# Two transposes moved from TensorE to DMA, statistics moved to ScalarE and a first chunk in halves, in a fused long-convolution and mixer kernel

## The chip, the core and the metric

The kernel runs on one core of a Trainium2 chip. The metric is the device time of one execution in microseconds (us). Several executions are timed on one chip, beside executions of the kernel before on the same chip. Each execution carries a state, fast or slow: slow, here, means that it was over 1.5% above the fastest of its own kernel. Ratios use fast executions alone and come with a 95% interval. A change counts as faster or slower when it is beyond 2%.

Names of engines: PE is TensorE (matmul), PEld its weight load, DVE VectorE, ACT ScalarE, POOL GpSimd, SP SyncE. In this kernel SP issues every DMA, so its program order is the order of all transfers.

## The reference

Two branches read the same `q`. Branch A is a long convolution of `k`, shifted and multiplied by `v`, with one filter of 2048 taps per channel (`ssm_k`, called h below). Branch B is a token mixer followed by a feed-forward network. S is 2048, D is 640, F is 1536; all is bf16.

```python
def _A_ref(q, k, v, shift_k, ssm_k, ssm_D):         # ssm_k: [D, S]
    ...                                              # k_shift: 4-tap shift of k
    kv = k_shift * v
    kv_f = rfft(pad(kv, 2*S));  kf_f = rfft(pad(ssm_k, 2*S))     # along S
    y = irfft(kv_f * kf_f)[:S] + kv * ssm_D
    return q * y
def _B_ref(x, w1, w2, w3, w4):
    h = gelu(layernorm(x) @ w1)
    ...                                              # 4 channel groups shifted by +1, -1, +2, -2 tokens
    x1 = x + hs @ w2
    return x1 + gelu(layernorm(x1) @ w3) @ w4
g = sigmoid((q * gate_w).sum(-1, keepdims=True))
out = g * _A_ref(...) + (1 - g) * _B_ref(q, ...)
```

## The kernel before

The kernel is written as a graph. Each node has a cost on the engines that can do it, its dependencies, and the buffers that it takes and gives back. A planner runs when the kernel is built: it simulates the graph with those costs, takes the ready node with the lowest key, and writes out one fixed order of instructions for each engine. On the chip every engine then works through its order; an instruction that is not ready holds all those behind it. The key is the longest path to the end plus a table of tuned shifts (`BIAS`).

```python
    def prepare(self):
        ...
            n.key = longest - n.rank + a + (b - a) * (k / (total[n.tag] - 1) if ... else 0.0)  # a, b from BIAS
    def forward(self):
        ...
                if n.bytes is not None:                      # a DMA: one line that all transfers share
                    line = max(now + 0.9, line) + n.bytes
                    fin = line + n.lat
                    ...
    def run(self):
        self.prepare()
        assert self.forward() is not None, "the plan is stuck"
        for n in sorted(self.nodes, key=lambda n: n.start):
            n.fn(n.engine)                                   # emitted once, in the planned order
SPILL = 3          # how many waiting copies let VectorE take one that ScalarE could do
BIAS = { ... }
```

The filter h arrives as [channel, time]; the transform wants time on the partitions. PE transposes it in five groups of 16, and ScalarE or VectorE copies each group out of PSUM:

```python
    for a in range(DT):                                       # DT = 5
        l_h.append(dma(lambda a=a: HNl[:, a, :], lambda a=a: hn_v[:, a, :], P * 4096, 4096, []))
    ...
        def f_ht(a=a, b=b):
            for t1 in range(T1):                              # T1 = 16
                nc.tensor.transpose(out=pt[:, t1 // 8, (t1 % 8) * P:(t1 % 8 + 1) * P], in_=HN[:, a, t1, :], identity=IDN[:])
        t = ten(pe(P, T1), [l_h[a], k_idn], f_ht, take=[b])
        ...                                                   # evac(...) copies to HT: the node k_ht
```

The table of the inverse transform (I1) is the transposed table of the forward one (F1), in 32 PE transposes:

```python
        def f_i1(h=h, b=b):
            for t1 in range(T1):
                nc.tensor.transpose(out=P16(b)[:, t1 // 8, (t1 % 8) * P:(t1 % 8 + 1) * P], in_=F1[:, t1, h, :], identity=IDN[:])
```

The statistics of the first normalization, one slab of 128 tokens at a time, are on VectorE. The first mixer product is 4 chunks of 512 tokens, five matmuls for each of five output tiles:

```python
            def f_st(s=s):
                for j in range(2):
                    nc.vector.bn_stats(out=BST[:, s % 4, j, :], in_=QX[:, s, j * DH:(j + 1) * DH])
                nc.vector.bn_aggr(out=MV[:, s, :], in_=BST[:, s % 4, :, :])
            ns.append(dvec(0.88, [l_q[s]], f_st))
    ...
                def f_w1(b=b, j=j, nt=n0 + j, xb=xb):
                    for k in range(DT):
                        nc.tensor.matmul(P32(b)[:, j, :], lhsT=lhsT, rhs=XNT[:, xb.slot, :, k, :], start=(k == 0), stop=(k == DT - 1))
```

The token shift of the mixer moves part of the activations between partitions' token slots by small DMAs (`mixsh`), and the last two of the ten matmuls of each slab of the second product (`W2`) read them.

Of the kernel before, what the change touches and what calls it, by code (L numbers as in the profile page):

```python
# [30 lines left out]
class Graph:  # L31
# [62 lines left out]
    def forward(self):  # L94
# [19 lines left out]
        while placed < len(nodes):  # L114
            while True:
                best = None
                for opts, q in queues.items():
# [5 lines left out]
                    if opts == "AV" and "A" not in es and len(q) + len(queues.get("A", ())) < self.spill:  # L123
                        continue
                    for item in sorted(q)[:24] if len(q) > 1 else q:
                        if all(len(free[p]) >= k for p, k in item[2].need):
                            if best is None or item[:2] < best[0][:2]:
                                best = (item, q, "A" if "A" in es else es[0])
                            break
# [51 lines left out]
SPILL = 3  # L181
BIAS = {
    "tA": (-1371, 329), "tF": (-1895.5, -724), "tM": (-895, -1806.5), "lq0": (-1748, -1584.5), "lq1": (-538.5, 1678),
    "lq2": (276.5, -148.5), "lq3": (-722.5, -2406.5), "lh0": (-599, -1171.5), "lh1": (-1262.5, 108), "lh2": (200, 76),
    "lh3": (-1543.5, -388), "lh4": (1371.5, 41), "lw1": (-813, 438.5), "lg5": (-966, -1374), "lsm": (933, 723.5),
    "halo": (630, 470), "lk0": (952.5, 1516.5), "lk1": (1326, -431.5), "lk2": (1247, 87.5), "lk3": (-844.5, -207.5),
    "lw2": (1010.5, 453), "pads": (-1392.5, -1903.5), "w1m": (-1378, -1422), "cj": (-2077.5, -1986.5),
    "hT0": (462, 872), "hT1": (-436.5, -54), "hT2": (-1567.5, -1321), "hT3": (-2415, -2453), "hT4": (-805, -1041),
    "LN1.4": (-1068.5, -2567), "LN1.5": (-1377.5, -101), "LN1.6": (1543, -177), "LN1.7": (694, 2098.5),
    "W1": (1173, 382), "W1.0": (-311.5, -391.5), "lv0": (930, 1060.5), "W1.1": (-908, -1017), "lv1": (2546.5, 2151),  # L190
    "W1.2": (-394.5, 484.5), "lv2": (-1163.5, -1804.5), "W1.3": (-365.5, 34.5), "lv3": (97.5, -194.5),
    "gate": (24.5, -1048.5), "mixsh": (-194.5, -1191.5), "W2": (-1393, -295.5), "ks": (-55, 124.5),
    "I1": (207.5, 486.5), "p0.1": (-514.5, -1036.5), "p0.gr": (-1858.5, -1351), "p0.2": (277.5, -1013),
    "p1.1": (85, -22.5), "p1.gr": (-1363.5, -97.5), "p1.2": (158, 494.5), "p2.1": (-1736.5, 232),
    "p2.hh": (-1426.5, -282), "p2.gr": (-1196.5, -1528), "p2.2": (43, -707), "p3.1": (242.5, 347),
    "p3.hh": (1072.5, 1036), "p3.gr": (-428.5, 985), "p3.2": (-2299.5, -1998), "qr": (-1357, -82),
    "inv0": (-194, 57.5), "inv1": (-1037.5, -824.5), "lw4": (-3682, -2611), "LN2": (-227, 584.5),
    "LN2.0": (-2078, -1915), "W3.0": (-910, -1875), "W4.0": (1205, 3183.5), "LN2.1": (-540.5, -382.5),
    "W3.1": (-347, 804.5), "W4.1": (545.5, 2369.5), "LN2.2": (-1716, -1532), "W3.2": (283, 624.5),
    "W4.2": (-1365, -2083.5), "LN2.3": (-1717.5, 551), "W3.3": (-793, 635.5), "W4.3": (1688.5, 488),  # L200
    "final": (-1560.5, -213.5),
# [11 lines left out]
def kernel(  # L213
# [47 lines left out]
    I1 = big.tile([P, 2, T1, P], BF16, name="I1")  # L261
# [9 lines left out]
    XD = dram.tile([4, T1, P, D], BF16, name="XD")  # L271
    HD = dram.tile([P + 64, T1, D], BF16, name="HD")
# [3 lines left out]
    HT = R3[:, 0].rearrange("p (e t d) -> p e t d", e=2, t=T1)  # L276
    KN = R3[:, 1].rearrange("p (t d) -> p t d", t=T1)
    HH = R3.rearrange("p a (t h d) -> p a t h d", t=T1, h=2)
    HN = R5.rearrange("p (a t2 t1) -> p a t1 t2", a=DT, t1=T1)
# [268 lines left out]


    k_ht = [[], []]  # L550
    for a in range(DT):
        G.tag = 'hT%d' % a
        b = G.buf("ps")

# [578 lines left out]
```

## Time and profile before

| before | us |
|---|---|
| median of 3 executions (lowest, highest) | 267.28 (266.84, 269.61) |
| the profiled execution, and its span | 265.0, 263.2 |
| PE busy, idle up to its last matmul at 259.24 | 237.3, 21.9 |
| first mixer matmul | 21.1 |
| first transform matmul that reads h | 29.8 |

The page of the profile first gives the busy time of each engine with its share of the span and its instructions, then strips of 40 slices (each 6.6 us) in which a digit is the busy share in tenths; `DMA` is the mean busy share of the 16 DMA engines. The line with percentages near the end is the chain of waits, followed back from the last instruction.

Windows of the kernel before. Columns: window, its length, then busy time and count of PE, PEld, DVE, ACT, POOL, then granted PE clock, DMA share, GB/s:

```profile
0.00:22.00 22.00, 9.13 (x73) 7.50 (x74) 19.77 (x66) 12.19 (x11) 15.49 (x35) 1.00 0.85 306
50.00:75.00 25.00, 24.05 (x183) 15.50 (x181) 23.25 (x40) 22.78 (x41) 7.83 (x18) 1.00 0.51 180
175.00:200.00 25.00, 23.57 (x149) 14.34 (x147) 10.25 (x13) 18.03 (x28) 0.00 (x0) 1.00 0.96 340
```

These three windows are the start, in which PE has 9.1 us of work; the middle of the mixer; and the third pass of the convolution.

The timeline of PE before. Columns: start, duration, engine, line, operation, output<-inputs, shapes, count; in brackets the idle time before it and what ended it:

```profile
7.09 1.93 PE L558 MATMUL ps_87<-IDN,R_71 128*128 128x128 bf16 x16 [7.09 <-DMA R_71<-in_A_ssm_k_dram]
...
21.10 2.84 PE L684 MATMUL ps_89<-XNT,R_75 128*128 128x512 bf16 x10
```

The first line is one of the five h groups of 16 transposes. It stands, with the next, in time in which PE has nothing else: of the 80 h transposes, part costs nothing. The last line is the start of the mixer.

### The profile page before, as it was taken

The numbers are of one execution on the slowest core, as the hardware profiler recorded it, in microseconds if no ns is written. First come the engines' busy times: TensorE is split into PE (matmuls) and PEld (weight loads), VectorE is DVE, ScalarE is ACT, GpSimd is POOL, SyncE is SP. The second block draws the span as 40 slices with busy tenths as digits, with TensorE's granted clock in tenths as the row PEclk, the third lists the DMA queues.
The fourth block names the chain that finished last, engine by engine and source line by source line (L and its number), as shares of the span: only waits on it lengthen the run. The fifth ranks groups of instructions, "written<-read, shape, count | busy, mean of one in ns | idle before, by whom it ended". The sixth has DMA issues, their size and how long they took to land.

```text
span 263.2 us, 4720 instructions
## 1 busy us (share of the span) xinstructions
PE 237.3 (90%) x1690; PEld 151.1 (57%) x1690; DVE 171.6 (65%) x340; ACT 184.3 (70%) x259; POOL 51.9 (20%) x115
## 2 busy tenths in 40 slices
PE   0549889999998899999999999997999999999993
PEld 0536446665665574555676555765556756756772
DVE  8999999889997799982111210364525444576995
ACT  2669969999889789989456789585877558753000
POOL 5894570061073585000000000000000000000000
PEclk9999999999999999999999999999999999999999
DMA  6994789944435996549899997999998572368874
GB/s 219 400 374 129 294 278 275 304 169 174 144 122 164 337 397 251 162 139 330 272 301 333 319 306 235 261 244 411 362 321 297 184 239 110 149 169 252 262 262 157
DMA packets 33601, 66.53 MB, mean 253 GB/s; under 512 B 5546, under 2 KB 22699, under 8 KB 33578
## 3 DMA queue, kind: packets, MB, share of 16 engines
q1 hardware_dynamic: 33578, 66.24, 76.3%
q8 instruction: 13, 0.21, 0.3%
q14 instruction: 10, 0.08, 0.1%
HBM read 40.79 MB, written 22.28 MB: 240 GB/s over the span
## 4 chain that ended last, share of the span: by engine, by line
PE 57%; DVE 16%; DMA 12%; ACT 7%; POOL 3%; issue 2%; SPq 1%; DVEq 0%; ACTq 0%
DMA VD<-HST 7%; PE ps_89 L1061 5%; PE ps_89 L1080 5%; DVE BST L590 4%; PE ps_88 L1061 4%; PE ps_90 L1080 4%; PE ps_90 L1061 4%; DMA XD<-SG 3%; DVE KV L990 3%; PE ps_90 L684 3%; PE ps_87 L1061 3%; ACT SG L351 2%; DVE QX L1097 2%; PE ps_87 L934 2%; PE ps_90 L780 2%
## 5 line engine op out<-in xcount | busy, mean ns | idle before, releaser
L1080 PEld LDWEIGHTS <-R_77 128*128 128x128 bf16 x384 | 37.6, 98 | 14.8
L923 DVE TENSOR_TENSOR PV<-XS,R_70 128x1280 bf16<-128x1280 bf16 x32 | 26.4, 824 | 28.4 <-PE ps_88 L934 12.0
L1061 PEld LDWEIGHTS <-R_75 128*128 128x128 bf16 x240 | 23.2, 98 | 21.0 <-issue 0.7
L809 DVE TENSOR_TENSOR R_72<-R_70,R_72 128x1280 bf16<-128x1280 bf16 (+3 forms) x32 | 23.9, 756 | 0.1
L1080 PE MATMUL ps_89<-R_72,R_77 128*128 128x320 bf16 x144 | 22.5, 299 | 0.0
L1080 PE MATMUL ps_90<-R_72,R_77 128*128 128x320 bf16 x144 | 21.8, 299 | 0.0
L812 DVE TENSOR_TENSOR R_72<-R_72 128x1280 bf16<-128x1280 bf16 x24 | 19.7, 823 | 0.5
L780 PEld LDWEIGHTS <-R_77 128*128 128x128 bf16 x160 | 15.6, 98 | 7.3 <-DMA R_77<-I_74 0.8
L1061 PE MATMUL ps_89<-XNT,R_75 128*128 128x512 bf16 x80 | 19.7, 379 | 0.0
L891 PEld LDWEIGHTS <-M_96 128*128 128x128 bf16 x128 | 12.3, 98 | 12.3 <-issue 2.7
L861 PEld LDWEIGHTS <-F_73 128*128 128x128 bf16 x128 | 12.1, 98 | 8.6 <-issue 2.3
L934 PEld LDWEIGHTS <-M_96 128*128 128x128 bf16 x128 | 12.5, 98 | 7.0 <-issue 1.5
L1090 DVE SCALAR_TENSOR_TENSOR QX<-ps_90,OMG,QX 128x640 bf16<-128x640 f32 x6 | 5.3, 880 | 17.0 <-PE ps_90 L1080 17.0
L684 PEld LDWEIGHTS <-R_75 128*128 128x128 bf16 x100 | 9.6, 99 | 10.1 <-issue 2.3
L351 ACT CAST HST<-ps_88 128x640 bf16<-128x640 f32 x14 | 9.7, 696 | 8.0 <-DMA VD<-HST 5.0
L1061 PE MATMUL ps_87<-XNT,R_75 128*128 128x512 bf16 x60 | 14.9, 379 | 0.2 <-ACT SG L351 0.2
L351 ACT CAST SG<-ps_88 128x640 bf16<-128x640 f32 x16 | 11.3, 703 | 4.7 <-PE ps_88 L861 3.6
L351 ACT CAST SG<-ps_87 128x640 bf16<-128x640 f32 x18 | 12.8, 709 | 2.4 <-DMA XD<-SG 1.2
L590 DVE BATCH_NORM_STATS2 BST<-QX 128x6 f32<-128x320 bf16 x32 | 13.7, 470 | 0.0
L351 ACT CAST SG<-ps_89 128x640 bf16<-128x640 f32 x17 | 12.1, 709 | 1.1 <-PE ps_89 L861 0.7
L1061 PE MATMUL ps_88<-XNT,R_75 128*128 128x512 bf16 x50 | 12.4, 379 | 0.2 <-ACT R_70 L353 0.2
L1061 PE MATMUL ps_90<-XNT,R_75 128*128 128x512 bf16 x50 | 12.4, 379 | 0.0
(182 smaller groups left out, 521.7 us busy)
## 6 DMA issues: line engine op xcount, KB each, us to landing
XD<-SG SPq DMA_DIRECT2D x64, 160.0 KB, 2.7
R_71<-XD SPq DMA_DIRECT2D x16, 640.0 KB, 5.9
VD<-HST SPq DMA_DIRECT2D x16, 320.0 KB, 4.6
R_70<-HD SPq DMA_DIRECT2D x8, 640.0 KB, 6.7
R_71<-in_A_ssm_k_dram SPq DMA_DIRECT2D x5, 512.0 KB, 6.8
R_70<-in_A_k_dram SPq DMA_DIRECT2D x4, 640.0 KB, 6.6
KV<-in_A_v_dram SPq DMA_DIRECT2D x4, 640.0 KB, 5.9
HD<-HST SPq DMA_DIRECT2D x8, 320.0 KB, 3.3
```

The costliest lines, as they stand in the source:

```text
L351: nc.scalar.copy(out=out(), in_=in_())
L590: nc.vector.bn_stats(out=BST[:, s % 4, j, :], in_=QX[:, s, j * DH:(j + 1) * DH])
L684: nc.tensor.matmul(P32(b)[:, j, :], lhsT=lhsT, rhs=XNT[:, xb.slot, :, k, :], start=(k == 0), stop=(k == DT - 1))
L780: nc.tensor.matmul(P32(b)[:, j, 0:DH], lhsT=gst_ap(k, s), rhs=W2[:, k, j * DH:(j + 1) * DH], start=(k == 0), stop=(k == DT - 1))
L809: lambda dst=dst, src=src, a=a, b=b, j=j, ds=ds: nc.vector.tensor_tensor(out=dst[:, a:b], in0=src, in1=CJ[:, j:j + 1, ds].to_broadcast([P, ...
L812: kprev = [dve(4 * DH, TWO, kprev, lambda dst=dst: nc.vector.tensor_tensor(out=ACC[:], in0=ACC[:], in1=dst[:], op=ALU.add))]
L861: nc.tensor.matmul(P32(b)[:, h, 0:DH], lhsT=F1[:, t1, h, :], rhs=src, start=True, stop=not dt)
L891: nc.tensor.matmul(P32(b)[:, h, 0:DH], lhsT=M3[:, 0, :], rhs=GRt[:, (4 * r + k // 4) % 3, k % 4, h, :], start=True, stop=True)
L923: k_pq[r, k] = dve(4 * DH, TWO, [n] + k_f1 + k_w2 + k_hh[r, k // 4], lambda xb=xb, vb=vb, k=k: nc.vector.tensor_tensor(out=PV[:, vb.slot], ...
L934: nc.tensor.matmul(P32(b2)[:, h, 0:DH], lhsT=M3[:, 1 + m, :], rhs=PV[:, vb.slot, m, h, :], start=(m == 0), stop=(m == 1))
L1061: nc.tensor.matmul(P32(b)[:, j, :], lhsT=W3[:, k, f * P:(f + 1) * P], rhs=XNT[:, xb.slot, :, k, :], start=(k == 0), stop=(k == DT - 1))
L1080: nc.tensor.matmul(P32(b)[:, j, 0:DH], lhsT=GTP[:, gbs[f // 4].slot, f % 4, i * P:(i + 1) * P], rhs=W4[:, f, j * DH:(j + 1) * DH], start=( ...
```

## The change

The intent is to take 112 transposes off PE, 13 us of PSUM copies off ScalarE, and some statistics off VectorE, and to let the mixer start when the first half of its first chunk is normalized. h is transposed by five DMA transposes while it is loaded. That leaves it in a layout that is not yet the one wanted, so it goes to DRAM (`HR`) and back, four stores and four loads. The table is transposed by one DMA. Four slabs get their sums from two accumulating passes on ScalarE. The order of sine and cosine angles is swapped. And the planner's spill rule and its whole `BIAS` table are new, so the fixed order of all engines is another one.

```diff
-SPILL = 3
+SPILL = 0.75       # the rule that uses it is new too: it counts time, not copies (cut)
 BIAS = {   # all 70-odd entries replaced (cut)
...
-        m, q = NANG[g % 2][:, 0:512], NANG[g % 2][:, 512:1024]
+        q, m = NANG[g % 2][:, 0:512], NANG[g % 2][:, 512:1024]
...
-        l_h.append(dma(lambda a=a: HNl[:, a, :], lambda a=a: hn_v[:, a, :], P * 4096, 4096, []))
+        l_h.append(G.dma(P * 4096 * 1.3, 4096 * 1.3, [], lambda a=a: nc.sync.dma_start_transpose(
+            out=HB[:, :, a * P:(a + 1) * P], in_=A_ssm_k[a * P:(a + 1) * P, :])))
...
-    k_ht = [[], []]             # 5 x 16 PE transposes and their copies (cut)
+    k_hr = [dma(lambda c=c: HR[4 * c:4 * c + 4].rearrange("b p d -> p b d"), lambda c=c: HB[:, 4 * c:4 * c + 4, :],
+                P * 5120, 1280, l_h, lat=0.6) for c in range(4)]
+    hr_v = HR.rearrange("b (q t) d -> (b q) t d", t=T1)
+    k_ht = [dma(lambda c=c: HT[:, 4 * c:4 * c + 4, :], lambda c=c: hr_v[:, 4 * c:4 * c + 4, :], P * 5120, 5120, k_hr)
+            for c in range(4)]
...
+    BY_ACT = (2, 3)             # pairs of slabs
+            def f_sta(s=s):
+                nc.scalar.activation(out=JK, in_=QX[:, s, :], func=ACT.Copy, scale=1.0 / D, accum_out=MV[:, s, 0:1])
+                nc.scalar.activation(out=JK, in_=QX[:, s, :], func=ACT.Square, scale=float(D ** -0.5), accum_out=MV[:, s, 1:2])
...
-            for j in range(1 if n0 == 4 else 2):
+            for i in range(2 if c == 0 else 1):       # chunk 0: two halves of 256 tokens
+                w = slice(2 * i, 2 * i + 2) if c == 0 else slice(0, 4)
+                for j in range(1 if n0 == 4 else 2):
...
-    k_i1 = []                   # 2 x 16 PE transposes and their copies (cut)
+    k_i1 = [G.dma(P * 8192 * 1.3, 8192 * 1.3, k_f1 + [...] + [k_ks[4]], lambda: nc.sync.dma_start_transpose(
+        out=I1.rearrange("p t h c -> p (t h) c"), in_=F1.rearrange("p t h c -> p (t h c)")))]
```

Each row of a transposed block that lands in `HB` is 128 values of bf16, so the destination is written in pieces of 256 bytes. In the planner's costs a DMA transpose is a copy with 1.3 times the bytes.

## The prediction

> **What bounds the kernel now.** TensorE. From counts and pipelined durations in the groups and the timeline: 340 matmuls of 512 columns at 216 ns (73 us), 992 of 320 columns at 136 ns (135 us), 160 layernorm transposes (14 us), 80 transposes of h (8.0 us), 32 of the inverse table (1.8 us), gate 2.5 us: 235 of the 263.2 us span, at clock 1.00. The chain of waits is 57% PE. The other 28 us are mainly the start: the first mixer matmul begins at 21.1 us; before it PE does three h groups of 1.9 us (two at 7.1 to 10.7, one at 19.4) and a few normalization transposes. From 20 to 100 us the windows show PE, VectorE and ScalarE all about 90% busy; from 100 us PE is dense to 259 us.
>
> **Removed.**
> - PE: h transposes (8.0 us), table transposes (1.8 us, near 97 us). The first two h groups (3.8 us) lie in idle start time, so 6 us is in the dense part.
> - ScalarE: h copies 9.4 us, table copies 3.7 us.
> - VectorE: statistics of four slabs, 4.4 us.
>
> **Added.**
> - ScalarE: four slabs x two accumulating passes of 0.74 + 0.19 us = 7.5 us; net -5.6 us.
> - GpSimd: about 1 us.
> - 25 more weight loads in chunk 0 (98 ns, overlapped).
> - DMA: h through DRAM and back (2.6 MB each way), 1 MB for the table. At the 400 GB/s of the busiest slices the round trip is an estimated 13 us, in the first 50 us, where the DMA share is already 0.7 to 1.0 in most windows. The Trainium skill, "DMA: Bandwidth & Descriptors", Latency and other measured facts, gives 261 GB/s for a DMA transpose with a non-contiguous middle dimension, as h's destination has; no trace here shows one yet. So the five h transposes take an estimated 10 us instead of 6.6.
>
> **On the critical path.** The 6 us of PE work: nearly all. The start: the first slabs' small operations end at 11.6 us, yet the first normalization starts at 15.5; with halves, fewer statistics on VectorE and no h copies on ScalarE, I expect the first mixer matmul at 17 to 18 us, 3 us earlier. Relief of ScalarE and VectorE before 100 us gives perhaps 1 us more. Against this: h is ready only at 45 to 50 us (first pass-1 matmul now at 29.8 us), so pass 1 no longer fills early gaps, and a DMA that lands late stalls a static schedule in order: I charge 2 us. Sum: 267.3 - 6 - 3 - 1 + 2 = about 259.5 us. Swapping sine and cosine costs no time.
>
> Predicted 259.5 us, range 250 to 271. Chances: faster by over 2% 0.57, within 2% 0.28, slower 0.15.
>
> **What would show it right or wrong.**
> - 112 fewer PE transposes; PE work, added up as above, near 225 us.
> - First mixer matmul before 18.5 us; at 20 or later the start gained nothing.
> - First pass-1 matmul on h at 45 to 50 us, without PE idle over 3 us between 20 and 50 us; a PE gap released by the h reload shows the round trip on the path.
> - h transposes landing in 5 to 12 us each, none holding the DMA queue's issue for long.
> - From 100 us PE as dense as before.
>
> **What would make it wrong.** DMA transposes several times slower than assumed, or blocking the issuing queue: then shift inputs, stores and reloads queue behind them and PE waits, near 97 us for the table as well; the time would be 270 or more. Or the new static order is better or worse for reasons unrelated to the listed parts. If the start gains 5 us and gaps before 100 us close too: 252.

## More of the kernel before

From the page of the kernel before:

```profile
span 263.2 us, 4720 instructions
PE 237.3 (90%) x1690; PEld 151.1 (57%) x1690; DVE 171.6 (65%) x340; ACT 184.3 (70%) x259; POOL 51.9 (20%) x115
...
PE   0549889999998899999999999997999999999993
...
DMA  6994789944435996549899997999998572368874
...
DMA packets 33601, 66.53 MB, mean 253 GB/s; under 512 B 5546, under 2 KB 22699, under 8 KB 33578
...
q1 hardware_dynamic: 33578, 66.24, 76.3%
...
PE 57%; DVE 16%; DMA 12%; ACT 7%; POOL 3%; issue 2%; SPq 1%; DVEq 0%; ACTq 0%
```

PE is busy for 90% of the span and makes up most of the chain. Its strip is thin in the first three slices and dense afterwards. The line `q1` is the queue of SP: its packets, megabytes, and share of the 16 engines' time, 76.3%. The DMA strip stands at 9 in many slices, near the start and in the second half above all: there is little free transfer time there. The clock strip (not shown) is 9 throughout.

In the third pass of the convolution half of the spectrum is a mirror image, made by eight DMAs from SBUF to SBUF (`hh`, 320 KB each). And the products of that pass are stored (`VD<-HST`) from a ring of two buffers (`hst`):

```python
            nc.tensor.matmul(P32(b)[:, j, 0:DH], lhsT=gst_ap(k, s), rhs=W2[:, k, ...], ...)   # k == 4: the tile the shifts fill
    ...
                k_hh[r, c].append(dma(lambda a=a, ks=ks: HH[a:a + 64, 1, ks]..., lambda a=a, ks=ks: HH[64 - a:128 - a, 0, ks]..., 64 * 5120, 5120, deps, lat=0.8))
    ...
            if k % 2 == 1:
                k_vd[dh, k // 2] = dma(lambda k=k: VD[dh]...[:, k - 1:k + 1], lambda hb=hb: HST[:, hb.slot]..., P * 2560, 2560, vfirst, lat=0.6, give=[hb])
```

## The result, and the profile after

| | before | after |
|---|---|---|
| executions, us | 269.61, 266.84, 267.28, 266.8 | 280.37, 279.66 (fast); 286.69, 287.1 (slow) |
| median, us | 267.06 | 283.53 |
| profiled span, us | 263.2 | 278.6 |
| last matmul ends, us | 259.24 | 274.85 |
| PE busy / idle until then, us | 237.3 / 21.9 | 234.3 / 40.6 |
| first mixer matmul, us | 21.1 | 22.6 |
| first transform matmul that reads h, us | 29.8 | 75.4 |

The ratio is 1.047, with a 95% interval of 1.038 to 1.056: slower. All ratios in this document are the mean time of one kernel's fast executions over the mean of the other's in the same rounds, so they are not quite the ratio of the medians that stand beside them. The two slow executions had a granted clock of 0.97, but so had the fast ones (0.975 and 0.982); why there are two groups the profile does not say, and nothing below rests on it.

The same lines of the page of the kernel after (one slice is now 7.0 us):

```profile
span 278.6 us, 4544 instructions
PE 234.3 (84%) x1603; PEld 147.1 (53%) x1603; DVE 169.5 (61%) x330; ACT 176.1 (63%) x264; POOL 50.3 (18%) x120
...
PE   0019899299889998789999899995799989899994
...
PEclk9999999789999999999999999999599999999999
DMA  7939899999969497988977999999978959565855
...
DMA packets 50096, 72.81 MB, mean 261 GB/s; under 512 B 20122, under 2 KB 39323, under 8 KB 50074
...
q1 hardware_dynamic: 50074, 72.53, 84.3%
...
PE 57%; DMA 15%; DVE 12%; ACT 8%; issue 3%; POOL 2%; SPq 2%; ACTq 0%; DVEq 0%; POOLq 0%
```

Every removed thing is gone (87 matmul instructions fewer: 112 transposes less 25 more mixer matmuls), ACT and DVE are lighter, and the time is longer. The strip of PE shows where: nothing in the first two slices, a 2 in the eighth slice, a 5 in the 28th; the clock strip dips beside them. The DMA engines moved 6.3 MB more: two times 2.62 MB for the round trip and 1.05 MB for the table. There are 14,576 more packets under 512 bytes (20,122 less 5,546), and the queue's share rose from 76.3% to 84.3%.

The windows after:

```profile
0.00:22.00 22.00, 2.06 (x17) 1.67 (x18) 19.83 (x65) 13.20 (x23) 17.43 (x43) 1.00 0.73 248
50.00:75.00 25.00, 19.80 (x161) 12.72 (x161) 17.53 (x35) 13.46 (x25) 9.13 (x18) 0.86 0.99 313
175.00:200.00 25.00, 19.98 (x130) 12.91 (x129) 10.60 (x13) 12.73 (x20) 0.00 (x0) 0.90 1.02 298
```

The start holds 7 us less PE work, and each of the other two windows some 4 us less. In the second window the DMA share doubled, from 0.51 to 0.99; in the third it was full before and is full now.

The account of the 15.6 us, from the PE timelines (start and end of every matmul) and the groups of PE instructions. The times of the groups overlap (before they add up to 287.6 us, where PE is busy for 237.3), so the rows of single groups are rough, and the fourth row is what closes the sum:

| term | us |
|---|---|
| PE busy: h transposes (8.1) and table transposes (2.2) gone | -10.3 |
| PE busy: first mixer product 25.1 to 27.8, 25 more matmuls in the halves | +2.7 |
| PE busy: the three groups that stand behind the two long gaps (L1052, L780, L882 of after) | +4.1 |
| PE busy: other groups and the overlap, which closes the sum | +0.5 |
| PE idle before the first mixer matmul, 12.9 to 20.4 | +7.5 |
| PE idle: two gaps, 5.21 at 49.3 us and 5.02 at 191.8 us | +10.2 |
| PE idle, other | +0.9 |
| sum | +15.6 |

So the removed work was really removed, and PE idle and a slower clock took back more than twice as much. Of the 7.5 us before the first mixer matmul, 1.5 us is the later start, and some 6 us is work that PE did there before: only some 4 of the 10.3 us lay behind that start. The 2.7 us of the halves is not a price of their instructions. At full clock, groups of five with 256 columns start 0.54 us apart (28.07 and 28.61), half of the 1.08 us of five with 512; but those from 24.18 to 27.38 start 1.07 us apart, at half that rate. The PE timeline after, at the start and at both gaps:

```profile
20.04 0.72 PE L623 MATMUL ps_89<-IDN,KV 128*128 128x128 bf16 x5 [11.23 <-DVE KV L615]
...
22.63 1.23 PE L683 MATMUL ps_91<-XNT,R_75 128*128 128x256 bf16 x5 [0.51 <-ACT XNT L351]
...
48.03 1.25 PE L780 MATMUL ps_89<-PV,R_77 128*128 128x320 bf16 x8
54.49 0.69 PE L780 MATMUL ps_89<-PV,R_77 128*128 128x320 bf16 x2 [5.21 <-DMA XD<-SG]
...
55.56 2.83 PE L780 MATMUL ps_90<-PV,R_77 128*128 128x320 bf16 x10
...
58.56 1.52 PE L780 MATMUL ps_89<-PV,R_77 128*128 128x320 bf16 x10
...
196.81 0.69 PE L882 MATMUL ps_89<-R_71,M_97 128*128 128x320 bf16 x2 [5.02 <-ACT HST L351]
197.41 2.29 PE L1052 MATMUL ps_88<-XNT,R_75 128*128 128x512 bf16 x5
```

*The first gap* cuts a slab of the second mixer product after eight of ten matmuls. The two that wait are those that read the tile which the token-shift DMAs fill. The profile names a store (`XD<-SG`) as the releaser. It is read here as one of several semaphores that came last in the record: a matmul does not read `XD`, and the code makes these two wait for the shift copies `R_77<-I_74`.

*After each gap* the same ten matmuls take 2.83 us instead of the 1.52 us three lines later, and five of 512 columns take 2.29 us where 1.24 us is the rule. The Trainium skill, "TensorE: Matmul & The Clock Gate", Part 1, says that PE falls to half its clock after an idle window of about 3.4 us and gets it back after as long a stretch of work. This trace agrees: both gaps are over 5 us, the clock strip reads 7 and 5 there, and the times nearly double. With the growth of the groups behind them (1.5 and 2.6 of the table's 4.1 us) the gaps cost some 6.7 and 7.6 us. But 3.4 us is no safe limit: in the experiments below the half rate also follows single gaps of 2.69 us (b_tab) and 2.29 us (no_trip_hh).

The queue of SP after, around the first gap and before the second. Same columns; the second number is how long the issue held the queue:

```profile
25.69 5.82 SPq L505 DMA_TRANSPOSE R_71<-in_A_ssm_k_dram  x1
...
37.65 3.97 SPq L505 DMA_TRANSPOSE R_71<-in_A_ssm_k_dram  x1
41.67 0.58 SPq L361 DMA_DIRECT2D R_70<-in_A_k_dram  x1
...
43.23 4.66 SPq L505 DMA_TRANSPOSE R_71<-in_A_ssm_k_dram  x1
47.99 2.59 SPq L361 DMA_DIRECT2D R_77<-I_74  x3
...
176.78 1.35 SPq L361 DMA_DIRECT2D R_70<-R_70  x2
...
180.22 2.39 SPq L361 DMA_DIRECT2D R_70<-R_70  x2
...
186.07 0.33 SPq L361 DMA_DIRECT2D VD<-HST  x1
```

An ordinary issue takes about 0.4 us; the five transposes held the queue for 2.13, 5.82, 2.10, 3.97 and 4.66 us, 18.7 us together. The shift copies stand behind the last. ScalarE wrote the last of their source at 41.3 us, and they were issued from 48.0 on.

*The second gap* begins with the same kind of queue. A part of the chain of waits after, of 185 to 200 us (start, duration, piece):

```profile
186.07 9.91 DMA VD<-HST
...
196.07 0.70 ACT HST L351
...
196.81 0.69 PE ps_89 L882 x2
```

The store issued at 186.07 takes 9.9 us to land, behind transfers that were issued before it (a reading that the fifth set below tests). Only then is one of the two `HST` buffers free, ScalarE can copy, PSUM is free, and PE goes on. Among the transfers before it are the mirror copies of the spectrum (`R_70<-R_70`). Before, their four pairs were spread out, issued at 141.0, 147.9, 163.0 and 167.6 us, and the first store of the pass (173.5 us) landed in 6.2 us. After, all four stand close together, at 166.2, 171.6, 176.8 and 180.2 us. The queue of SP before, at the last pair and the first store, and that store in the chain of waits:

```profile
167.64 1.10 SPq L361 DMA_DIRECT2D R_70<-R_70  x2
...
173.49 0.33 SPq L361 DMA_DIRECT2D VD<-HST  x1
...
173.49 6.22 DMA VD<-HST
```

*The start.* The first normalization is at 19.5 us (15.5 before). The scale and shift of the first two slabs were ready at 15.9 us. Then VectorE's fixed order first had three other slabs' statistics (one of them under way) and the making of a small table. The first two normalized slabs were not asked for as early as the halves would have allowed. And the three h groups that PE did here before (some 5.5 us) are gone.

### The profile page after: what moved, and what is told of

It is laid out like the page before. It is cut to its first block, busy times and chain, and to the rows that moved or that the text cites. A ratio compares the mean times of both kernels' runs of the same rounds, so it can differ in the third digit from the quotient of the medians.

```text
span 278.6 us, 4544 instructions
## 1 busy us (share of the span) xinstructions
PE 234.3 (84%) x1603; PEld 147.1 (53%) x1603; DVE 169.5 (61%) x330; ACT 176.1 (63%) x264; POOL 50.3 (18%) x120
## 2 busy tenths in 40 slices
DMA packets 50096, 72.81 MB, mean 261 GB/s; under 512 B 20122, under 2 KB 39323, under 8 KB 50074
## 3 DMA queue, kind: packets, MB, share of 16 engines
q1 hardware_dynamic: 50074, 72.53, 84.3%
## 4 chain that ended last, share of the span: by engine, by line
PE 57%; DMA 15%; DVE 12%; ACT 8%; issue 3%; POOL 2%; SPq 2%; ACTq 0%; DVEq 0%; POOLq 0%
DMA XD<-SG 10%; PE ps_90 L1071 7%; PE ps_89 L1071 5%; PE ps_88 L1052 5%; DMA VD<-HST 4%; PE ps_88 L1071 4%; PE ps_88 L683 2%; PE ps_91 L1071 2%; PE ps_91 L1052 2%; PE ps_90 L1052 2%; PE ps_89 L1052 2%; ACT XNT L351 2%; DVE R_72 L809 2%; PE ps_89 L882 2%; ACT SG L351 2%
## 5 line engine op out<-in xcount | busy, mean ns | idle before, releaser
L1071 PEld LDWEIGHTS <-R_77 128*128 128x128 bf16 x384 | 37.5, 98 | 15.5 <-issue 0.4
L1052 PEld LDWEIGHTS <-R_75 128*128 128x128 bf16 x240 | 23.6, 100 | 24.1 <-issue 3.9
L780 PEld LDWEIGHTS <-R_77 128*128 128x128 bf16 x160 | 15.9, 101 | 13.9 <-issue 6.8
L1052 PE MATMUL ps_88<-XNT,R_75 128*128 128x512 bf16 x80 | 21.8, 406 | 1.3 <-ACT SG L351 1.3
L1071 PE MATMUL ps_90<-R_72,R_77 128*128 128x320 bf16 x144 | 22.2, 299 | 0.2 <-DVE QX L1081 0.2
L882 PEld LDWEIGHTS <-M_97 128*128 128x128 bf16 x128 | 12.4, 99 | 18.4 <-issue 9.8
L683 PEld LDWEIGHTS <-R_75 128*128 128x128 bf16 x125 | 12.9, 107 | 8.9 <-issue 1.1
L1052 PE MATMUL ps_89<-XNT,R_75 128*128 128x512 bf16 x70 | 17.4, 379 | 0.2 <-ACT SG L351 0.2
L351 ACT CAST SG<-ps_91 128x640 bf16<-128x640 f32 x21 | 14.7, 699 | 3.8 <-PE ps_91 L852 2.8
L852 PEld LDWEIGHTS <-F_73 128*128 128x128 bf16 x128 | 12.4, 98 | 8.5 <-issue 1.9
L925 PEld LDWEIGHTS <-M_97 128*128 128x128 bf16 x128 | 12.5, 98 | 6.6 <-issue 1.3
L615 DVE TENSOR_SCALAR XY<-QX,RS_109,MB_110 128x640 bf16<-128x640 bf16 x16 | 7.1, 444 | 13.0 <-PE ps_91 L623 12.1
L1052 PE MATMUL ps_90<-XNT,R_75 128*128 128x512 bf16 x60 | 14.7, 379 | 0.0
L1071 PE MATMUL ps_89<-R_72,R_77 128*128 128x320 bf16 x96 | 14.7, 299 | 0.0
L780 PE MATMUL ps_89<-PV,R_77 128*128 128x320 bf16 x60 | 9.5, 304 | 5.2 <-DMA XD<-SG 5.2
L351 ACT CAST SG<-ps_89 128x640 bf16<-128x640 f32 x16 | 11.3, 709 | 4.0 <-DMA XD<-SG 2.0
L683 PE MATMUL ps_88<-XNT,R_75 128*128 128x512 bf16 (+1 forms) x60 | 13.5, 359 | 0.3 <-ACT XNT L351 0.3
L882 PE MATMUL ps_89<-R_71,M_97 128*128 128x320 bf16 x42 | 9.4, 306 | 5.0 <-ACT HST L351 5.0
```

Of the source, the lines that this page charges most:

```text
L351: nc.scalar.copy(out=out(), in_=in_())
L615: n = dve(D, FAST, [small] + after + k_xn[-1:], lambda s=s, src=src: nc.vector.tensor_scalar(out=src(), in0=QX[:, s, :], scalar1=rs[:, s:s ...
L683: nc.tensor.matmul(P32(b)[:, j, w.start * P:w.stop * P], lhsT=lhsT, rhs=XNT[:, xb.slot, w, k, :], start=(k == 0), stop=(k == DT - 1))
L852: nc.tensor.matmul(P32(b)[:, h, 0:DH], lhsT=F1[:, t1, h, :], rhs=src, start=True, stop=not dt)
L882: nc.tensor.matmul(P32(b)[:, h, 0:DH], lhsT=M3[:, 0, :], rhs=GRt[:, (4 * r + k // 4) % 3, k % 4, h, :], start=True, stop=True)
L925: nc.tensor.matmul(P32(b2)[:, h, 0:DH], lhsT=M3[:, 1 + m, :], rhs=PV[:, vb.slot, m, h, :], start=(m == 0), stop=(m == 1))
```

## The experiments

The theories, at the outset:

- *The transposing issue.* The DMA transposes hold SP's queue; what stands behind them is late.
- *The DMA load.* What costs is the traffic: 256-byte pieces, the round trip, fuller engines, whatever instruction makes it.
- *The order.* The new static plan is worse for reasons that have nothing to do with the moved operations: crowded transfers near 185 us, the late start.
- *The small parts.* The table or the statistics cost by themselves.

All the kernels below passed the comparison with the reference, those too that put wrong data into h or into the inverse table. So the comparison, with these inputs, does not see such errors in branch A, and none of these runs says whether the swap of sine and cosine is right. Unless said otherwise a kernel was timed in three rounds, those of the fourth and fifth set in five. The kernels of one set ran on one chip; each set is set against its own executions of the kernel before, whose medians were 269.46, 268.64, 269.37, 266.90 and 268.07 us.

### First set: which part costs

**plain_h.** The five DMA transposes become plain copies in the same 256-byte pieces. h is wrong; order and bytes are unchanged.

```diff
-        nc.sync.dma_start_transpose(out=HB[:, :, a * P:(a + 1) * P], in_=A_ssm_k[a * P:(a + 1) * P, :])
+        nc.sync.dma_start(out=HB[:, :, a * P:(a + 1) * P], in_=A_ssm_k[a * P:(a + 1) * P, :].rearrange("p (b d) -> p b d", b=T1))
```

> The kernel after, with the five transposing loads of h replaced by plain loads of the same bytes into the same places (in pieces of 256 bytes; wrong result on purpose). Order of all engines unchanged. Theory 1 (the issue of a transposing DMA holds the one issuing queue, 18.7 us in five issues, and so delays the mixer shift copies; PE then idles 5.2 us at 49 us and runs at half clock after it): each load's issue falls below 1 us, the PE gap at 49 us is gone, time 271 to 275 us, ratio to before about 1.02. Rival 2 (the round trip's traffic and the order of the new plan): issue may fall, but the gap or an equal one stays and the time is 278 to 283 us, ratio 1.04 to 1.05.

Measured: 283.04 us, ratio 1.069 (1.050 to 1.088). Not faster than the change. The queue of SP in plain_h:

```profile
36.17 0.60 SPq L505 DMA_DIRECT2D R<-in_A_ssm_k_dram  x1
36.81 4.31 SPq L361 DMA_DIRECT2D R<-in_A_k_dram  x1
...
42.76 6.84 SPq L361 DMA_DIRECT2D R<-I  x3
```

The copies of h are now issued in 0.6 us, and the next DMA in the queue is held in their place: the k load for 4.31 us, the three shift copies for 6.84. PE still has a gap of 3.98 us at 49.1 and one of 5.68 at 192.4. The theory of the transposing issue falls. What is held is whatever stands in the queue behind these transfers; a transposing issue is merely one place where the hold shows. The Trainium skill, "Advanced Engine Details and Errata", X-Bar Transpose (TRN2), says that transpose DMAs are as fast as regular ones. Against copies in the same pieces this agrees: the transposes landed in 4.4 us (median), these copies in 5.2.

**h_first.** The transposes go ahead of the mixer's weights, the store of h ahead of the shift copies, the reload where the store was.

```diff
-        for n in sorted(self.nodes, key=lambda n: n.start):
+        new = {"lh": at("lw2") - 0.01, "hst": at("mixsh") - 0.01, "hld": at("hst") - 0.005}
+        for n in sorted(self.nodes, key=lambda n: new.get("lh" if n.tag[:2] == "lh" else n.tag, n.start)):
```

> The kernel after, right result, order of PE, VectorE, ScalarE and GpSimd unchanged; only the issuing queue is reordered: the five transposing loads come before the first W2 load, for which that queue stood idle from 4.9 to 16.5 us, and store and reload of h move forward with them. Theory 1: the issues, still some 4 us each, now lie in that idle stretch, the shift copies leave on time, the PE gap at 49 us is gone, time 271 to 275 us. Rival 2: 278 us or more. The PE gap at 192 us (a store of V that takes 9.9 us to land) is left in both theories.

Measured: 298.5 us, ratio 1.115 (1.088 to 1.142), far from what was expected. SP's queue in h_first, and nothing else in that time:

```profile
6.70 21.35 SPq L505 DMA_TRANSPOSE R<-in_A_ssm_k_dram  x5
```

Five transposes in a row hold the queue for 21.35 us, for 2.62 MB: 123 GB/s, while the DMA engines are full (share 1.05, 249 GB/s in all from 6 to 28 us, with the loads that were already under way). PE then stands still from 30.7 to 46.5 us. (This profiled execution was a slow one.) The Trainium skill, "DMA: Bandwidth & Descriptors", Latency and other measured facts, gives 261 GB/s for a DMA transpose whose middle dimension is not contiguous. Here the transposes' own share was half of that, beside other loads; no run here has a transpose alone.

**b_tab.** The kernel before, in its own order, with the inverse table by DMA.

```diff
-            for t1 in range(T1):
-                nc.tensor.transpose(out=P16(b)[...], in_=F1[:, t1, h, :], identity=IDN[:])
+            if h == 0:
+                nc.sync.dma_start_transpose(out=I1.rearrange("p t h c -> p (t h) c"), in_=F1.rearrange("p t h c -> p (t h c)"))
```

> The kernel before with the table transpose alone done by DMA, in the order of before. PE loses 1.8 us near 97 us, ScalarE 3.7 us. Theory 1: one issue of about 4.9 us near 97 us delays stores of pass 1 by that much, but PE has mixer work queued: gain 0 to 2 us, ratio 0.993 to 1.00. If the delayed stores stall PE: 1.00 to 1.02.

Measured: 270.83 us, ratio 1.021 (1.006 to 1.036). A line of SP's queue in b_tab:

```profile
99.06 6.61 SPq L825 DMA_TRANSPOSE I<-F  x1
```

and one of PE's timeline:

```profile
112.73 1.24 PE L1060 MATMUL ps<-XNT,R 128*128 128x512 bf16 x5 [2.83 <-ACT HST L353]
```

The issue of 1 MB holds the queue for 6.6 us. A spectrum load and stores stand behind it, and PE waits 2.83 us at 109.9. But most of what this profile loses is not the table's. PE had waited before, for a load of h, and then ran at half clock:

```profile
49.12 1.40 PE L558 MATMUL ps<-IDN,R 128*128 128x128 bf16 x16 [2.69 <-DMA R<-in_A_ssm_k_dram]
50.31 2.87 PE L780 MATMUL ps<-PV,R 128*128 128x320 bf16 x10
```

When the table's DMA is issued, at 99.06 us, PE is already 3.5 us behind the kernel before (the same ten matmuls start at 94.79 there and at 98.26 here); at the end it is 4.6 us behind. So what the table costs in this order is not shown; only that nothing is gained. (The five matmuls after the gap of 2.83 us take 1.24 us, no half clock, though the ten after the shorter one take 2.87 instead of 1.52.)

**b_stats.** The kernel before, in its own order, with the four slabs' sums on ScalarE.

```diff
-            ns.append(dvec(0.88, [l_q[s]], f_st))
+            ns.append(dvec(0.88, [l_q[s]], f_sta if p in BY_ACT else f_st))      # f_sta: two activations with accum_out
```

> The kernel before with the statistics of slabs 4 to 7 alone moved to ScalarE, in the order of before. VectorE loses 4.4 us before 30 us, ScalarE gains 7.5 us, while it still copies h. If the start is bound by VectorE: 1 to 3 us faster, ratio 0.99. If ScalarE, busy with h copies, is as tight: 1 to 3 us slower, ratio 1.005 to 1.01.

Measured: 275.59 us, ratio 1.030 (1.005 to 1.056). That is slower than either expectation. New PE gaps of 1.96 and 2.62 us stand at 27 to 36 us, ended by VectorE's normalization; three more, of 1.75 to 2.28 us, stand at 53, 164 and 188 us. The interval is wide, and two of the four executions were slow. What is safe to say is that this part gains nothing when the order is not made for it.

### Second set: what of h's path costs

**no_trip.** No transposes and no round trip; the reload reads h itself as rows (wrong values). Same order.

```diff
-        nc.sync.dma_start_transpose(out=HB[...], in_=A_ssm_k[a * P:(a + 1) * P, :])
+        None
-    k_hr = [dma(lambda c=c: HR[...], lambda c=c: HB[...], P * 5120, 1280, l_h, lat=0.6) for c in range(4)]
+    k_hr = [G.dma(P * 5120, 1280, l_h, lambda: None, lat=0.6) for c in range(4)]
-    hr_v = HR.rearrange("b (q t) d -> (b q) t d", t=T1)
+    hr_v = A_ssm_k seen as rows of 640                    # (the rearrange is cut)
```

> The kernel after, order of PE, VectorE, ScalarE and GpSimd unchanged, with h's transposing loads and the store to DRAM left out and the reload reading the input h itself in its 5120-byte rows (as if h came transposed; wrong result on purpose). Theory 3 (the data rate: 256-byte pieces of h at some 123 GB/s and the round trip fill the DMA queues before 75 us, whatever sends them): the mixer shift copies leave early, the PE gap at 49 us is gone, pass 1 on h is not waited for, time 262 to 270 us, ratio 0.98 to 1.01. Rival 2 (the new static order loses by itself): 274 us or more, ratio over 1.03, with the late start (first mixer matmul near 22 us) and the gap near 192 us both left.

Measured: 275.45 us, ratio 1.024 (1.006 to 1.042); two of the four executions were slow. The gap at 49 us is gone, which shows that h's transfers made it. But the time is well above the kernel before. PE of no_trip:

```profile
183.32 1.25 PE L1071 MATMUL ps<-R,R 128*128 128x320 bf16 x8
190.36 0.69 PE L882 MATMUL ps<-R,M 128*128 128x320 bf16 x2 [5.79 <-ACT HST L351]
```

The second gap stays, 5.79 us, where the chain of waits has a store that took 10.80 us to land, though h's transfers were over long before; and the first mixer matmul is still at 22.6 us. Something that is not h's way in costs half of the loss or more (1.024 here, 1.034 in no_trip_qr below, of 1.047).

**no_pieces.** h is copied in rows of 4096 bytes (wrong values); the round trip stays.

```diff
-        nc.sync.dma_start_transpose(out=HB[:, :, a * P:(a + 1) * P], in_=A_ssm_k[a * P:(a + 1) * P, :])
+        nc.sync.dma_start(out=R5[:, a * 2048:(a + 1) * 2048], in_=A_ssm_k[a * P:(a + 1) * P, :])
```

> The kernel after with h loaded plainly in rows of 4096 bytes and then stored to DRAM and reloaded as after does (wrong result on purpose); order of all engines unchanged. If the 256-byte pieces alone are the cost: as the run without the round trip, 264 to 271 us. If the round trip of 5.2 MB matters as well: in between, 270 to 276 us. Rival 2: 278 us or more.

Measured: 277.05 us, ratio 1.039 (1.027 to 1.051). The packets and the issues of h (count, size of each, median us to landing) from the page and the list of DMAs of no_pieces, and a line of its SP queue:

```profile
DMA packets 40416, 72.81 MB, mean 265 GB/s; under 512 B 9802, under 2 KB 29003, under 8 KB 40394
...
R<-in_A_ssm_k_dram SPq DMA_DIRECT2D x5, 512.0 KB, 4.1
...
40.78 2.12 SPq L361 DMA_DIRECT2D R<-I  x3
```

As many bytes as after, half of the packets under 512 bytes, and the gap at 49 us is gone: the three shift copies, issued at 48.0 us in the change, leave at 40.8. So it is the small pieces that made that gap: plain copies in 256-byte pieces have it (plain_h), copies in long rows have not. The Trainium skill, "DMA: Bandwidth & Descriptors", Specifications, asks for at least 512 bytes for the full rate; that agrees, as far as the gap shows it. A gap of 6.43 us at 186.6 stays. The time shows little of it: 1.039 against 1.047, and these come from two sets.

**plain_tab.** The table's transpose becomes a plain copy (a wrong table).

```diff
-        nc.sync.dma_start_transpose(out=I1.rearrange("p t h c -> p (t h) c"), in_=F1.rearrange("p t h c -> p (t h c)"))
+        nc.sync.dma_start(out=I1.rearrange("p t h c -> p (t h c)"), in_=F1.rearrange("p t h c -> p (t h c)"))
```

> The kernel after with the table's transposing DMA replaced by a plain copy of the same bytes in rows of 8192 bytes (wrong result on purpose), order unchanged. The transposing issue took 4.9 us at 98 us, where PE stayed busy. If it costs: 1 to 3 us faster than the kernel after, and the issue under 1 us. If not: within 1 us of it (280 to 284 us).

Measured: 284.63 us, ratio 1.064 (1.040 to 1.088), with gaps of 4.00 us at 49.3, 2.65 at 185 and 4.40 at 195. The copy is issued in 0.54 us, and nothing is gained. In this order the table's transpose is not what costs.

### Third set: orders searched afresh

If the order is the fault, an order made for the change should remove it. The kernel's own planner was used, with twelve minutes of search in the `BIAS` table for each of four kernels.

```diff
 BIAS = {   # before_s: before;  after_s: after, planner told 4.27 us per h transpose and 4.9 us for the table
-    ...
+    ...    # rest_s: after, but h on PE as before;  hs_s: halves and four slabs alone, h and table on PE
```

before_s is the control: what such a search gives to the kernel that needs none.

> Control: the operations of before, unchanged, with the bias table of its planner searched afresh for 12 minutes (the same search as for the three kernels beside it). Theory 2 (each static order has its own misses on the chip, whatever the operations): the new order differs from before by up to 3% either way. If orders of equal planned length run equally on the chip: within 1% of before, 265 to 270 us.

> The operations of after, right result, with the measured issue times of the transposing DMAs (4.27 us for each part of h, 4.9 us for the table) given to the planner and its bias table searched afresh. Theory 3 (the DMA path of h costs by itself, even in an order made for it): slower than the control by 1.5 to 3%, 270 to 277 us. Theory 2 (only the order was bad): equal to the control or faster, 260 to 268 us.

> The change without its h part: table by DMA (4.9 us given to the planner), first mixer chunk in halves, four slabs' sums on ScalarE; h on TensorE as before; bias table searched afresh. If the h part is the one that costs: 0 to 1.5% faster than the control, 262 to 268 us. If the table or the slabs cost too: 1% or more slower than the control.

> Halves and the four slabs' sums on ScalarE alone, h and table on TensorE as before; bias table searched afresh. Against the run beside it this tells what the table's DMA is worth: if it gives its 1.8 us of PE and 3.7 us of ScalarE, this kernel is 1 to 2 us slower than that one; against the control, what halves and slabs are worth: 0 to 1% faster expected.

| searched afresh | us | ratio (95%) |
|---|---|---|
| before_s: nothing changed | 269.1 | 1.008 (0.995 to 1.021) |
| hs_s: halves and slabs | 266.2 | 0.993 (0.978 to 1.008) |
| rest_s: halves, slabs and table | 272.06 | 1.017 (1.008 to 1.027) |
| after_s: all, h by DMA too | 274.98 | 1.026 (1.010 to 1.042) |

The order seems to be a large part. The whole change, in one order made with honest DMA costs, loses 2.6% (1.0 to 4.2) and not 4.7%. But it does not win, and in these four orders each further step of moving work to DMA measured worse; the fourth set shows how much of that an order alone can do. (after_s's profiled execution was a slow one; it had a gap of 6.47 us at 188.2, released by a spectrum load.) A search of this length does not find the order of the kernel before again (1.008), so differences below about 1% between searched kernels say little. (before_s keeps the old spill rule; the other three have the new one.)

### Fourth set: the second gap, the table, the scatter of orders

What stayed open was why the gap near 185 us remains without h, whether rest_s lost by the table or by its order, and how much two searches differ.

**no_trip_qr.** no_trip, with the last two reloads of q, which stand in the queue near 175 us, moved behind the gap.

```diff
-        for n in sorted(self.nodes, key=lambda n: n.start):
+        late = dict(zip([n for n in self.nodes if n.tag == "qr"][2:], (190.0, 198.0)))
+        for n in sorted(self.nodes, key=lambda n: late.get(n, n.start)):
```

> The kernel after without h's transposing loads and round trip (wrong result on purpose, as the run without the round trip), all orders kept, but the last two reloads of q are issued some 20 us later, away from the copies of the spectrum of h and the first stores of V. Theory (the PE gap of 5 to 6 us near 185 to 192 us, seen in every kernel with after's order, is the DMA queue crowded by that order): gap under 2 us, no half clock after it, 6 to 8 us faster than without this edit, ratio to before 0.99 to 1.00. Rival (the copies and reads of the spectrum alone fill the queue): gap of 4 us or more stays, ratio 1.02 to 1.03.

Measured: 274.96 us, ratio 1.034 (1.027 to 1.040), with a gap of 5.72 us at 182.9. The q reloads are not the cause. The run is also the best measure of no_trip itself, for nothing that counts has changed: 1.024 and 1.034 are two readings, on two chips, of nearly one kernel.

**rest_notab.** The order of rest_s with the table's DMA left out; a memset on GpSimd fills the table (wrong).

```diff
-    ... nc.sync.dma_start_transpose(out=I1..., in_=F1...)
+    ... nc.gpsimd.memset(I1, 0.5)
```

> The replanned kernel with table, halves and slabs (h on TensorE), order kept, with the table's DMA left out and the table's place filled by GpSimd instead (wrong result on purpose). If the table's DMA is what made that kernel 2.4% slower than the one with halves and slabs alone: ratio to before 0.99 to 1.00. If its order is: ratio stays at 1.01 to 1.02.

Measured: 269.69 us, ratio 1.0135 (1.008 to 1.019), where rest_s had 1.017 in its set. The two differ by 0.4%, less than sets may be off by: no cost of the table's DMA is seen in that order, and without it the loss stays.

**rest_s2** and **hs_s3** are second orders for the operations of rest_s and hs_s, from another search.

> The operations of the replanned kernel with table, halves and slabs, another search of the bias table (other seed, planned length within 0.6 us of the first). If two orders of equal planned length run equally, ratio 1.01 to 1.02 as the first; if the order's own misses are 1% or more, the two differ by that: 0.99 to 1.03.

> The operations with halves and slabs alone (h and table on TensorE), another search of the bias table (other seed). If halves and slabs are worth something by themselves: 0.985 to 1.00 as in the first order. If the first order was lucky: 1.00 to 1.02.

Measured: rest_s2 268.05 us, ratio 1.008 (1.003 to 1.014); hs_s3 266.95 us, ratio 1.006 (1.000 to 1.013). Against the first orders (1.017 and 0.993) that is a scatter of about 1% between two orders of the same operations. In hs_s3 the first mixer matmul starts at 11.9 us, 9 us earlier than in the kernel before, and the time is no better. A start gained at the front is not carried to the end when the order behind it does not use it.

### Fifth set: the mirror copies, and the best version again

**no_trip_hh** and **after_hh.** In no_trip and in the kernel after, the last two pairs of mirror copies of the spectrum go behind the first and the second store of the third pass.

```diff
+        vd = [n for n in self.nodes if n.tag == "p2.2" and n.bytes]; hh = [n for n in self.nodes if n.tag == "p2.hh"]
+        late = {hh[4]: vd[0].start + 0.01, hh[5]: vd[0].start + 0.02, hh[6]: vd[1].start + 0.01, hh[7]: vd[1].start + 0.02}
-        for n in sorted(self.nodes, key=lambda n: n.start):
+        for n in sorted(self.nodes, key=lambda n: late.get(n, n.start)):
```

> The kernel after without h's transposing loads and round trip (wrong result on purpose), all orders kept, but the last two of the four pairs of copies that mirror the spectrum of h (320 KB each, 7 to 10 us to land, four pairs within 15 us in this order) are issued behind the first and the second store of V. If these copies crowd the queue so that the store of V lands 10 us late: the PE gap of 5.8 us near 185 us falls under 2 us, no half clock after it, ratio to before 0.99 to 1.01 instead of 1.02 to 1.03. If the gap stays or turns into a wait of VectorE for the mirrored copy of the same length: ratio 1.02 to 1.035.

> The kernel after, right result, with the same two pairs of copies issued later. If they make the gap near 192 us: gap under 2 us, 5 to 8 us faster than the kernel after, 272 to 276 us, ratio 1.02 to 1.035; the gap at 49 us stays. If not: 280 us or more.

Measured: no_trip_hh 271.33 us, ratio 1.013 (1.006 to 1.021). PE of no_trip_hh, where the gap was (this profiled execution was a slow one; the gaps, not the times, are what is read):

```profile
197.76 1.69 PE L1072 MATMUL ps<-R,R 128*128 128x320 bf16 x8 [1.81 <-ACT HST L352]
```

The gap of 5.8 us is gone; the largest that are left are 1.81 and 2.29 us, both followed by matmuls at half rate (the granted clock was 0.52 from 229 to 232 us). The crowd of mirror copies in front of the stores made it, by the order alone: four issues moved, no operation changed.

after_hh measured 279.34 us, ratio 1.044 (1.037 to 1.051). The first store, now issued in front of the moved copies, landed in 3.8 us instead of 9.9, which shows the crowd at work; the two behind them took 9.1 and 9.5. The gap at 192 became 2.27 us at 198.7 and 1.74 at 235, and the gap at 49 us, of 5.41, stayed, as it should. Expected were 5 to 8 us, and at most 1 us is seen between 1.047 and 1.044, which come from two chips. The windows of the two profiles show where it went: PE idle between 165 and 205 us fell from 5.0 to 2.4 us, but after 205 us it rose from 1.7 to 3.4. Why these later waits grew was not tested.

**hs_s_again** is hs_s, the best version, once more.

> The replanned kernel with halves and slabs alone, run again in 5 rounds since it is the only one that came out below before (0.9934, interval 0.978 to 1.008). If that was real: 0.985 to 0.997 with an interval below 1. If it was the chip's scatter: 0.997 to 1.01.

Measured: 265.4 us, ratio 0.995 (0.989 to 1.000): within 2%, and at the edge of what five rounds can tell from nothing. It is the fastest found. It keeps h and the table on TensorE.

### The runs together

| run | ratio (95%) | what it says |
|---|---|---|
| after | 1.047 (1.038 to 1.056) | |
| plain_h | 1.069 (1.050 to 1.088) | not the transposing, but pieces and load |
| plain_tab | 1.064 (1.040 to 1.088) | the table's transposing is not it |
| h_first | 1.115 (1.088 to 1.142) | an earlier h is worse |
| no_pieces | 1.039 (1.027 to 1.051) | without small pieces the first gap is gone |
| no_trip, no_trip_qr | 1.024 (1.006 to 1.042), 1.034 (1.027 to 1.040) | without h's path; second gap stays |
| no_trip_hh | 1.013 (1.006 to 1.021) | and with the mirror copies later; second gap gone |
| after_hh | 1.044 (1.037 to 1.051) | mirror copies later, h's path kept |
| b_tab, b_stats | 1.021 (1.006 to 1.036), 1.030 (1.005 to 1.056) | single parts in an order not made for them |
| before_s | 1.008 (0.995 to 1.021) | control of the searches |
| hs_s, again, hs_s3 | 0.993, 0.995, 1.006 | halves and slabs: about nothing |
| rest_s, rest_s2, rest_notab | 1.017, 1.008, 1.0135 | table: about nothing, or a little worse |
| after_s | 1.026 (1.010 to 1.042) | all of it in an order made for it: still a loss |

## Why the prediction was wrong

The prediction was 259.5 us, faster; the result was 283.53 us, slower.

- *"The 6 us of PE work: nearly all [on the critical path]."* This is the step that failed. The work did go: 10.3 us by the groups, with some 6 us of it, not 3.8, in the time before the first mixer matmul. But PE was on the path only because its inputs came in time, and what replaced the work was transfers on DMA engines that were already busy for 76% of the span. Their load rose to 84%, and PE's idle time rose by 18.6 us. The prediction added up PE work; it should have asked which transfers would be late.
- *"I charge 2 us"* for a DMA that lands late. This term was sized far too small. The first gap alone was 5.2 us and some 1.5 us at half clock. Taking h's path away was worth 1.3 to 2.3% (1.047 to 1.034 or 1.024), an estimated 3.5 to 6 us. In an order searched with honest costs it still cost about 1 to 2% (1.026 against the 1.017 and 1.008 of two orders without it), which is not clear of the scatter of about 1% between orders.
- *"None holding the DMA queue's issue for long"* and the transposes' *"estimated 10 us"*. They landed in 4.2 to 6.1 us (median 4.4), at the low end of the 5 to 12 expected or below, but the five held the queue for 18.7 us. The list of what could be wrong named this: "then shift inputs, stores and reloads queue behind them and PE waits." It happened to the shift inputs, at 49 us. Its explanation, that transposing blocks the issue, was tested and fell: plain copies in the same pieces block what is behind them just as well (plain_h), long rows do not (no_pieces).
- *"h is ready only at 45 to 50 us".* The first transform matmul on h came at 75.4 us. The store was issued at 53.5 us and the reload from 66.7 us on. The pass was filled by other work, and h itself caused no gap.
- *"First mixer matmul at 17 to 18 us, 3 us earlier".* Measured 22.6 us, 1.5 us later. The inputs of the first normalization were there at 15.9 us; the fixed order of VectorE put other work first. The halves could not help what the order did not ask for. The 25 more matmuls themselves cost nothing at full clock, as predicted (0.54 us for five, half of the 1.08 of the wider ones).
- *"From 100 us PE as dense as before".* It was not: 5.0 us at 191.8, and half clock after it. The gap is the new order's. no_trip has it without h's transposes and round trip, and no_trip_hh loses it when two pairs of copies move. The prediction mentioned an order that is "better or worse for reasons unrelated" only as a risk and gave it no term in the sum. Without h's path it is worth 1 to 2% (no_trip_hh); in the whole change, moving the same copies brought at most 0.3% (after_hh).
- *Right:* 87 matmul instructions fewer (112 less 25), PE's work at about 225 us by the same counts (the measured busy time fell by 3.0 us only), and that the swap of sine and cosine costs no time that can be seen (hs_s has it, at 0.993 and 0.995).

*Settled:* h's small pieces make the first gap; the crowded mirror copies make the second. *Likely:* the table and the sums gain nothing, since no order that was tried shows a gain clear of the noise; and the whole change loses in an order made for it too, by 2.6% (1.0 to 4.2) in the one order that was searched. *Open:* how the loss divides between pieces and round trip (no_pieces and no_trip differ by 0.5 to 1.5%, and the intervals overlap); why the later waits of after_hh grew; and how much the late start costs by itself, since what is left in no_trip_hh (1.3%) was not taken apart and hs_s3's early start gained nothing. The sets ran on different chips, so ratios of different sets may be off by up to about 1% against each other.

## What to carry to other kernels

Before work is moved from a full engine to DMA, look at the DMA share of the windows where it would go and at the length of the pieces that it will be written in: the table's transpose saved 2.2 us of matmul time, kept the one issuing queue for 4.9 to 6.6 us, and brought no gain in any order tried. In a kernel with a static order an edit and its order are one change, so test the edit in an order made for it and put a re-planned, unchanged kernel beside it: here that control alone moved by 0.8%. PE idle can cost more than its length: here the half clock came after every gap in mid-kernel of 3.9 us or more, and after some of about 2 us.

## What the Trainium skill lacked or had wrong

- "DMA: Bandwidth & Descriptors": 261 GB/s for a DMA transpose with a non-contiguous middle dimension held for no transpose here. Five in a row, beside loads under way, moved 2.62 MB in 21.35 us, 123 GB/s; a single one of 0.52 MB landed in 4.4 us (median, 4.2 at the least, which is 125 GB/s). None ran without other transfers beside it.
- "Advanced Engine Details and Errata", X-Bar Transpose (TRN2): "as fast as regular DMAs" holds for the time to landing (4.4 us, against 5.2 us for copies in equally small pieces and 4.1 us for rows of 4096 bytes), but says nothing of what waits behind: with the rows the PE gap of 5.2 us goes away.
- No page says how long a DMA_TRANSPOSE of this size holds the queue that issues it on this chip ("DMA: Bandwidth & Descriptors" has sequencer cycles only in a table about a later chip, with a column for earlier ones): its issue took 2.1 to 5.8 us in the change for 0.52 MB and 4.9 and 6.6 us for 1.05 MB, where an ordinary issue took about 0.4 us; and with plain copies in small pieces the hold moves to the next DMA in the queue (4.3 and 6.8 us).
- No page that was read has the latency of a 320 KB store behind a crowded queue: 9.9 us and 10.8 us where the median of its kind is 4.6 us in the kernel before.
- "TensorE: Matmul & The Clock Gate": the half clock after an idle window of about 3.4 us agrees for long gaps (5.21 and 5.02 us, then 2.83 and 2.29 us for what takes 1.52 and 1.24), but shorter ones did not always escape: after 2.69 us (b_tab) and 2.29 us (no_trip_hh) the granted clock was 0.50 and 0.52, while after 2.83 us (b_tab) it stayed 1.00.
